# Making w_out's seven operands during attention and the middle experts instead of inside the w_in stage

## The chip, the cores and the metric

The kernel runs on one core of one Trainium2 chip. The metric is the device time of one execution in microseconds (us), as the median of several executions. In the trace of a core PE is the matrix engine (PEld are its weight loads), DVE is VectorE, ACT is ScalarE, POOL is GpSimd, and SP is the queue from which most DMAs are issued.

## What is computed

Three blocks follow each other on 2304 tokens (4 batches of 576). In float32:

```python
def phi(x):                                   # attention, 8 heads of 64, 128 features
    proj = np.einsum('bhsd,md->bhsm', x, omega)
    h = proj - np.sum(x * x, axis=-1, keepdims=True) / 2.0
    return np.exp(h - np.max(h, axis=-1, keepdims=True)) / np.sqrt(m)
kv  = np.einsum('bhsm,bhsd->bhmd', k_p, v);  z = np.sum(k_p, axis=2)
x   = einsum(q_p, kv) / (einsum(q_p, z)[..., None] + 1e-06)
# mixture of experts, top 1 of 8, 512 -> 1024 -> 512
out[mask] = gate_w[mask, None] * (np.maximum(x[mask] @ w1[e], 0.0) @ w2[e])
# dense block, 512 -> 2048 -> 512; w_in and w_out come as 64-bit floats
h = x @ w_in
y = (h * (1.0 / (1.0 + np.exp(-1.702 * h)))) @ w_out
```

## The kernel before

**Attention and experts (to about 405 us).** Attention goes through eight quads (a batch and four heads). Its matrix products hand their results to DVE and ACT and wait for what these return, so PE is kept full with the matmuls of an expert (lines 679 to 764, tiles `m_ps` and `w_ps`) that are laid between them. Each batch goes to one expert, the commonest choice of its tokens. The expert's weights are split into a high and a low part: `wh` by ACT and `wl` by POOL (line 662, `wl<-st,wh`); for the last batch `wl` is made on DVE. DVE makes the low part of the hidden layer (line 697, `h1l`) and scales the result (line 745), and SP stores it to `y_dram`.

**The dense block** uses a seven-product scheme for both matmuls. `first` (line 1068) runs the w_in stage: 24 groups, one for each of eight column pairs j of w_in and each of three sets t of 768 tokens, with seven products of six matmuls each. Its operands are `wi` (two halves of seven combinations of w_in, made by `prep_ins`, line 867) and `y` (the same for a set of tokens, made by `prep_y`, line 929). GELU results go to `g_dram` through three `ob` buffers. `second` (line 1161) runs the w_out stage: nine blocks of 256 tokens, each with seven products of 24 matmuls in the order 1, 7, 5, 6, 2, 4, 3. Its weights `p`, `pw` come from `prep_w` (line 1129), which reads `wo_dram` and splits what it reads. `wo_dram` is filled by `prep_outs` (line 903): for each of eight j it loads two blocks of w_out in 64-bit floats, decodes each with three DVE instructions (line 786), makes four differences (`O_MIX`), and stores seven operands. That is ten DVE instructions for each j. Its results are the tile `pz`, and it begins once set 2 of y exists (line 1260).

**What sets the order.** A `Runner` (line 819) steps the side jobs (`prep_y`, `prep_ins`, `prep_outs`, `prep_w`) once for each step of the main program; the number that a job yields is how many steps it rests. `behind(ins, n)` (line 113) ties an instruction behind the last n ones recorded on its engine, so it stays where it was recorded. All else a scheduler orders by a timeline that it models; after that each engine runs its list in order, and so does the SP queue.

**Room.** `xep` holds the inputs of even batches. `ly` (raw w_in, `yt`, `y0`) is taken when attention has released `att`; `wp` (dec, `wi0`, `wi1`) when batch 2 has passed its first layer. After the last w_in group `wq` takes `wp`'s place and gives two of the five homes `gs` in which `second` keeps its split operands. `marked` (line 1063) records three small matmuls that touch three PSUM banks before the w_in stage.

Of the kernel before, what the change touches and what calls it, by code (L numbers as in the profile page):

```python
# [22 lines left out]
def kernel(  # L23
# [29 lines left out]
    OUT_PACE = 9  # L53
    OUT_GAP = 1
# [152 lines left out]
    xep = tc.alloc_tile_pool(name="xep", bufs=1, side="right")  # L207
    att = tc.alloc_tile_pool(name="att", bufs=1)
# [470 lines left out]
    def moe_gen(b):  # L679
# [3 lines left out]
        for hf in range(2):  # L683
# [46 lines left out]
            for dt in range(KD):  # L730
# [13 lines left out]
                y = yq.tile([P, NH], F32, tag="y", name="y", bufs=3)[:, 0:HS]  # L744
# [122 lines left out]
    def prep_ins():  # L867

        def load(n, j):
            return load_raw(slots["ly"], 0, j + n * NP, 4 if j < 2 else 0)  # L870

        raw = [load(0, 0), load(1, 0)]
        yield IN_PACE
        for j in range(NP):
# [16 lines left out]
            pool, tag = slots["wi"][j % 3]  # L891
            t = pool.tile([P, 14 * HALF], F32R, tag=tag, name="wi", bufs=1)
            w = t.rearrange("p (s o c) -> p s o c", s=2, o=7)
            for o, x in ((slice(0, 2), dec[:, 0:2]), (slice(2, 4), dec[:, 2:4]), (slice(4, 7), mix[:, 0:3])):
                split(w[:, 0, o], w[:, 1, o], x, HOLD)
                yield 1
            wi_t[j] = (w[:, 0], w[:, 1])
# [5 lines left out]
    def prep_outs():  # L903

        raws = slots["raw_o"]

        def load(n, j):
            f = j + n * NP
            nc.sync.dma_start(out=raws[n], in_=w_out[f * P:(f + 1) * P, :])

        load(0, 0)
        load(1, 0)
        yield OUT_PACE
        for j in range(NP):
            z = slots["z"][:, j % 2]
            zi = z.bitcast(I32)
            for n in range(2):
                yield from decoding(zi[:, 2 * n:2 * n + 2].rearrange("p a c -> p (a c)"), raws[n])
                if j + 1 < NP:
                    load(n, j + 1)  # L920
# [3 lines left out]
            nc.sync.dma_start(out=wo_dram[0, :, j], in_=z[:, 0])  # L924
            nc.sync.dma_start(out=wo_dram[1:7, :, j].rearrange("o p d -> p o d"), in_=z[:, 2:8])
            outs[0] += 1
            yield OUT_GAP

# [32 lines left out]
    if True:  # L961
# [11 lines left out]
        done_a = done_m = 0.0  # L973
        a_live = True
# [9 lines left out]
        while a_live:  # L984
# [11 lines left out]
            tick()  # L996
        att_done[0] = True
# [8 lines left out]
        ly = tc.alloc_tile_pool(name="ly", bufs=1)  # L1006
        slots["ly"] = ly
        wp = None
        jobs = Runner(4)
# [8 lines left out]
        y0 = set_tile(ly, 0)  # L1018
        jobs.queue.append(prep_y(0, [y0], 4))
        for n, c in enumerate(Mg):  # L1020
            tick()
            if wp is None and x_done[0] >= B - 1:
                flush()
                xep.release()
                wp = tc.alloc_tile_pool(name="wp", bufs=1)
# [12 lines left out]
        slots["wi"].append((hp, "wi2"))  # L1038
# [24 lines left out]
        def marked(tag):  # L1063

            ps = bank_of(tag, 1, NH)
            nc.tensor.matmul(out=ps, lhsT=y_t[0][0][:, 0, 0, 0:P], rhs=y_t[0][0][:, 0, 0])

        def first(j, t):
# [27 lines left out]
            qs = yq.tile([P, NH], F32, tag="y", name="qs", bufs=3)  # L1096
# [64 lines left out]
        def second(k, gt):  # L1161
            a11, a12, a21, a22 = (gt[:, h, :, i * P:(i + 1) * P] for i in range(2) for h in range(2))

            def made(out, x, y, op):
                behind(nc.vector.tensor_tensor(out=out, in0=x, in1=y, op=op), HOLD if k < 2 else 0)
# [8 lines left out]
            def product(n, ps, start, gs):  # L1174
                gh, gl = gs
                w = wo_t[n]
                for f in range(NP):
                    for m, (x, i) in enumerate(((gh, 0), (gh, 1), (gl, 0))):
# [4 lines left out]
                        if k < 2 and f + m == 0:  # L1183
# [16 lines left out]
            ops = {1: halves_of(a11, HOLD if k < 2 else 0)}  # L1200
# [8 lines left out]
            ops[5] = halves_of(s1)  # L1209
            pa = bank_of("a", 3, HD)  # L1210
# [3 lines left out]
            made(s1, s1, a11, ALU.subtract)  # L1214
            ops[6] = halves_of(s1)
# [43 lines left out]
        def after_group(j, t):  # L1259
            if "z" not in slots and 2 in y_t:  # L1260
                p = ly.tile([P, ZW], F32, tag="yt", name="pz", bufs=1)
                slots["z"] = p[:, 0:16 * HD].rearrange("p (a o d) -> p a o d", a=2, o=8)
                raw = hp.tile([P, DM], I64, tag="raw", name="raw_o", bufs=1)
                slots["raw_o"] = [p[:, 16 * HD:16 * HD + 2 * DM].bitcast(I64), raw]
                jobs.queue.append(prep_outs())
            if (j, t) == (7, 0):
                p = ly.tile([P, SETW], F32R, tag="y0", name="p0", bufs=1)
                jobs.queue += [prep_w(0, p[:, 0:WO], 14), prep_w(1, p[:, WO:2 * WO], 18)]
# [11 lines left out]
            if (j, t) == (5, 2):  # L1280
                jobs.queue.append(prep_w(4, hp.tile([P, WO], F32R, tag="wi2", name="pw", bufs=1), 10))
            if (j, t) in ((7, 1), (5, 2)):
                for _ in range(2):
                    next(blocks[0])
# [25 lines left out]
        jobs.queue += [prep_w(5, p[:, 0:WO], 4, 0), prep_w(6, p[:, WO:2 * WO], 5, 0)]  # L1310
# [20 lines left out]
        ly.release()  # L1331

# [119 lines left out]
```

## Time and profile before

| | |
|---|---|
| median of 3 runs | 788.24 us (787.06 to 791.26) |
| profiled execution, its own time | 792.79 us |
| its span | 790.9 us |
| PE busy | 751.5 us (95%) |
| DVE, ACT, POOL busy | 524.1, 339.6, 131.2 us |

PE is busy nearly throughout, so the time is PE's work plus what PE loses: stretches in which it waits, and stretches in which its clock is granted at half. Where these lie is to be read stage by stage: attention with experts to about 405 us, the w_in stage to 592.8 us, then the w_out stage.

### The profile page before, as it was taken

Reading aid. Unit: us, or ns where it says so; the run is one execution under the profiler, and the core shown is the slowest. Engines: PE = TensorE matmul, PEld = TensorE weight load, DVE = VectorE, ACT = ScalarE, POOL = GpSimd, SP = SyncE. Lnnn points to the kernel's source line nnn. Section 1 sums busy time; section 2 is a strip of 40 time slices with the busy share of each in tenths; the row PEclk is TensorE's granted clock in tenths of the full one; section 3 lists DMA queues with packets and bytes.
Section 4 is the critical chain, followed back from the end, with each engine's and each line's share of the span. In section 5 each row is a group of like instructions: output and inputs, shape, how many; then the busy total and the mean of one; then the engine's idle time right before and its main releaser. Section 6 shows DMA issues by size and latency. Waiting matters only on the chain.

```text
span 790.9 us, 14445 instructions
## 1 busy us (share of the span) xinstructions
PE 751.5 (95%) x5589; PEld 724.4 (92%) x5589; DVE 524.1 (66%) x1178; ACT 339.6 (43%) x643; POOL 131.2 (17%) x78
## 2 busy tenths in 40 slices
PE   7998899999999999799999999998998899999996
PEld 6877799998999999799999999988997899999996
DVE  5877786567764453563679578794267778777761
ACT  5545663345323341541255544443565334444430
POOL 3555386258102240000000000000000000000000
PEclk9999999999999999999999999999999799999998
DMA  6455865267513321644237399896779334444211
GB/s 159 124 142 151 238 185 151 63 177 192 129 32 125 104 65 49 196 125 146 85 109 279 117 314 319 301 316 216 285 259 333 107 128 147 132 135 132 76 27 31
DMA packets 135724, 126.59 MB, mean 160 GB/s; under 512 B 57568, under 2 KB 120288, under 8 KB 134752
## 3 DMA queue, kind: packets, MB, share of 16 engines
q1 hardware_dynamic: 128736, 106.72, 45.0%
q10 hardware_dynamic: 6912, 18.88, 6.3%
q8 instruction: 46, 0.75, 0.4%
q14 instruction: 30, 0.25, 0.1%
HBM read 78.69 MB, written 40.39 MB: 151 GB/s over the span
## 4 chain that ended last, share of the span: by engine, by line
PE 68%; DMA 11%; DVE 11%; ACT 4%; issue 3%; SPq 1%; POOL 1%; ACTq 0%; DVEq 0%; POOLq 0%
PE m_ps L126 17%; PE qa L1179 12%; PE qa L1078 9%; PE qm L1179 6%; PE w_ps L126 4%; DMA g_dram<-g 3%; PE pb L1179 3%; PE num L431 3%; DMA m<-in_k_dram 2%; PE qm L1078 2%; PE qu L1078 2%; PE kv_ps L389 2%; DMA st<-in_moe_w_dram 2%; DMA m<-in_q_dram 1%; PE pr L331 1%
## 5 line engine op out<-in xcount | busy, mean ns | idle before, releaser
L1078 PE MATMUL qa<-y,wi 128*128 128x384 f32 x576 | 110.6, 339 | 3.7 <-DVE g L863 2.3
L1078 PEld LDWEIGHTS qa<-y,wi 128*128 128x128 f32 x576 | 100.8, 188 | 6.9 <-DVE g L863 4.0
L126 PE MATMUL m_ps<-xh,wh 128*128 128x288 f32 x256 | 79.5, 311 | 4.3 <-DVE h1l L697 4.3
L126 PE MATMUL m_ps<-xh,wl 128*128 128x288 f32 x256 | 77.2, 302 | 0.0
L126 PE MATMUL m_ps<-xl,wh 128*128 128x288 f32 x256 | 77.1, 301 | 0.0
L662 POOL TENSOR_TENSOR wl<-st,wh 128x1024 fp32r<-128x1024 f32 x23 | 54.5, 2377 | 90.8 <-ACT wh L660 90.7
L697 DVE SCALAR_TENSOR_TENSOR h1l<-m_ps,h1h 128x288 fp32r<-128x288 f32 x64 | 29.0, 455 | 61.2 <-ACT h1h L694 60.9
L346 DVE TENSOR_REDUCE small<-pr 128x4 f32<-128x512 f32 (+1 forms) x80 | 51.1, 639 | 13.9 <-PE pr L338 6.7
L660 ACT ACTIVATE wh<-st 128x1024 fp32r<-128x1024 f32 (+1 forms) x33 | 33.9, 1033 | 47.8 <-DMA st<-in_moe_w_dram 23.4
L126 PEld LDWEIGHTS m_ps<-xh,wh 128*128 128x128 f32 x256 | 49.2, 192 | 5.2 <-DVE h1l L697 4.7
L694 ACT ACTIVATE h1h<-m_ps 128x288 fp32r<-128x288 f32 x64 | 25.8, 405 | 59.9 <-PE m_ps L126 59.8
L126 PEld LDWEIGHTS m_ps<-xl,wh 128*128 128x128 f32 x256 | 49.3, 193 | 0.1
L126 PEld LDWEIGHTS m_ps<-xh,wl 128*128 128x128 f32 x256 | 49.2, 192 | 0.0
L126 PE MATMUL m_ps<-h1h,wh 128*128 128x288 f32 x160 | 48.5, 304 | 0.0
L126 PE MATMUL m_ps<-h1l,wh 128*128 128x288 f32 x160 | 47.8, 299 | 0.0
L126 PE MATMUL m_ps<-h1h,wl 128*128 128x288 f32 x160 | 47.5, 298 | 0.0
L1179 PE MATMUL qa<-p,p 128*128 128x256 f32 x360 | 46.8, 288 | 0.0
L1179 PE MATMUL qa<-p,gs 128*128 128x256 f32 x360 | 45.6, 282 | 1.1 <-DVE gs L817 0.8
L1179 PEld LDWEIGHTS qa<-p,p 128*128 128x128 f32 x360 | 45.5, 196 | 0.0
L1179 PEld LDWEIGHTS qa<-p,gs 128*128 128x128 f32 x360 | 43.9, 189 | 1.5 <-DVE gs L817 1.0
L431 PE MATMUL num<-kv,qpT 128*128 128x65 f32 (+1 forms) x320 | 39.0, 265 | 2.2 <-ACT qpT L419 1.4
L431 PEld LDWEIGHTS num<-kv,qpT 128*128 128x128 f32 (+1 forms) x320 | 36.2, 183 | 5.4 <-ACT qpT L419 2.7
(211 smaller groups left out, 1823.8 us busy)
## 6 DMA issues: line engine op xcount, KB each, us to landing
g_dram<-g ACTq DMA_DIRECT2D x48, 384.0 KB, 4.2
st<-in_moe_w_dram SPq DMA_DIRECT2D x31, 512.0 KB, 3.9
pg<-g_dram SPq DMA_DIRECT2D x10, 1024.0 KB, 5.7
raw<-in_moe_w_in_dram SPq DMA_DIRECT2D x16, 512.0 KB, 4.9
gt<-g_dram SPq DMA_DIRECT2D x8, 1024.0 KB, 6.1
wo_dram<-pz SPq DMA_DIRECT2D x8, 768.0 KB, 4.9
p<-wo_dram SPq DMA_DIRECT2D x6, 1024.0 KB, 7.2
yt<-y_dram SPq DMA_DIRECT2D x12, 384.0 KB, 5.7
```

The source lines that it names most:

```text
L126: ins = nc.tensor.matmul(out=ps, lhsT=a, rhs=b, start=start and n == 0, stop=stop and n == 2)
L331: nc.tensor.matmul(out=ps[:, :, h2], lhsT=xT[:, (2 * pr + h2) * 2 + t0 // 2], rhs=wbd)
L346: nc.vector.tensor_reduce(out=pm, in_=ps[:, :w], axis=AX.X, op=ALU.max, negate=on_act)
L389: nc.tensor.matmul(out=kv_ps[:, h, :], lhsT=kp[j // 2][:, j % 2, h2, :], rhs=vm[:, h, t, :], start=(t == 0), stop=False,)
L431: nc.tensor.matmul(out=ps[:n, c, h2, :], lhsT=lhsT, rhs=kv[:, h, :])
L660: nc.scalar.activation(out=hi[:, :, s], in_=st[:, :, s], func=ACTF.Copy)
L662: eng.tensor_tensor(out=lo[:, :, s], in0=st[:, :, s], in1=f32(hi)[:, :, s], op=ALU.subtract)
L694: nc.scalar.activation(out=hh[:, f], in_=ps, func=ACTF.Relu)
L697: nc.vector.scalar_tensor_tensor(out=hl[:, f], in0=ps, scalar=0.0, in1=f32(hh[:, f]), op0=ALU.max, op1=ALU.subtract)
L1078: ins = nc.tensor.matmul(out=ps, lhsT=w[:, a, ks], rhs=y[:, b, kk], start=start and kk + m == 0, stop=kk == 1 and m == 2, skip_group_check ...
L1179: ins = nc.tensor.matmul(out=ps, lhsT=x[:, f], rhs=w[i][:, f], start=start and f + m == 0, stop=f == NP - 1 and m == 2, skip_group_check=True,
```

## The change

`prep_outs` now runs during attention and the experts of batches 0 to 2, from the moment batch 0 has passed its first layer. It has a pool `wz` of its own (tags a and b, 16 KB of each partition), one operand tile instead of two, loads tied to places in SP's list, and a rest of 5 steps after each j. Since `wz` takes room, `ly` is allocated only when `xep` is released; `prep_y` of set 0 therefore starts when batch 2 has passed its first layer and all expert weights are staged, and `prep_ins` waits for `prep_outs`. `wz` later holds `wi` of j = 0, 3, 6, and then two of the homes `gs`, which are so free one group before the w_in stage ends. In the first w_out block the sixth operand is made before product 1 is issued (`sixth`), and two more steps of the block are taken after group (6, 2). `prep_w` rests shorter (14, 18, 10, 4, 5 become 10, 14, 7, 3, 4). The third w_out block is tied in order as the first two are. `marked` is tied behind the matmul before it; `y` becomes a tile of 288 columns, and `qs` moves to a pair of buffers in `hp`.

```diff
-    OUT_PACE = 9
-    OUT_GAP = 1
+    OUT_PACE = 5
+    IN_FIRST = 5
...
+    wz = tc.alloc_tile_pool(name="wz", bufs=1)
     att = tc.alloc_tile_pool(name="att", bufs=1)
...
     def prep_ins():
...
+        while outs[0] < NP:
+            yield 1
         raw = [load(0, 0), load(1, 0)]
-        yield IN_PACE
+        yield IN_FIRST
...
     def prep_outs():
-        raws = slots["raw_o"]
+        z = wz.tile([P, 8 * HD], F32, tag="a", name="z", bufs=1).rearrange("p (o d) -> p o d", o=8)
+        zi = z.bitcast(I32)
+        raws = wz.tile([P, 2, DM], I64, tag="b", name="raw_o", bufs=1)
         def load(n, j):
             f = j + n * NP
-            nc.sync.dma_start(out=raws[n], in_=w_out[f * P:(f + 1) * P, :])
+            behind(nc.sync.dma_start(out=raws[:, n], in_=w_out[f * P:(f + 1) * P, :]), 2)
...
-        yield OUT_PACE
+        yield 8
         for j in range(NP):
-            z = slots["z"][:, j % 2]
-            zi = z.bitcast(I32)
             for n in range(2):
...
-            for o, a, b, op in O_MIX:
+            for i, (o, a, b, op) in enumerate(O_MIX):
+                if j + 1 < NP and not i % 2:
+                    load(i // 2, j + 1)
                 behind(tt(nc.vector, z[:, o], z[:, a], z[:, b], op), HOLD)
                 yield 1
...
-            yield OUT_GAP
+            yield OUT_PACE
...
+        jobs = Runner(4)
+        jobs.queue.append(prep_outs())
...
             tick()
+            if x_done[0]:
+                jobs()
...
-                slots["wi"] = [(wp, "wi0"), (wp, "wi1")]
+                slots["wi"] = [wi_pair, wi_home(wp, "wi1")]
...
-                slots["go"] = jobs.queue.extend([prep_ins(), prep_y(1, home1, 4)])
+                slots["go"] = jobs.queue.extend([prep_y(0, [set_tile(ly, 0)], 4), prep_ins(), prep_y(1, home1, 4)])
...
+            def sixth():
+                made(s1, s1, a11, ALU.subtract)
+                ops[6] = halves_of(s1)
+            if not k:
+                yield
+                sixth()
+                yield
             pa = bank_of("a", 3, HD)
             product(1, pa, True, ops[1])
             c1 = kept(pa, "c1")
             yield
-            made(s1, s1, a11, ALU.subtract)
-            ops[6] = halves_of(s1)
+            if k:
+                sixth()
...
+            if (j, t) == (6, 2):
+                gs_homes.extend(wz.tile([P, GSW], F32R, tag=tag, name="gs", bufs=1) for tag in ("a", "b"))
...
-        gs_homes += [wq.tile([P, GSW], F32R, name=f"gs{i}") for i in range(2)]
```

Three places show how the lists of the engines moved.

DVE, the first decoding of w_out in the changed kernel (`z` and `raw_o` are its tiles; `small`, `mx`, `qp`, `kp` belong to attention). The kernel before has at this place:

```order
L367 TENSOR_TENSOR kp<-pr,mx 128x512
L346 TENSOR_REDUCE small<-pr 128x4
L355 TENSOR_TENSOR small<-small,sq 128x4
L355 TENSOR_TENSOR mx<-small,sq 128x4
L367 TENSOR_TENSOR qp<-pr,mx 128x512
```

and the changed kernel:

```order
L368 TENSOR_TENSOR kp<-pr,mx 128x512
L347 TENSOR_REDUCE small<-pr 128x4
L789 TENSOR_SCALAR z<-raw_o 128x512
L356 TENSOR_TENSOR small<-small,sq 128x4
L794 SCALAR_TENSOR_TENSOR z<-raw_o,z 128x512
L356 TENSOR_TENSOR mx<-small,sq 128x4
L798 SCALAR_TENSOR_TENSOR z<-raw_o,z 128x512
L368 TENSOR_TENSOR qp<-pr,mx 128x512
```

One instruction on `z` now stands between nearly every two of attention's. PE's list answers to this: the same transposes of attention stand behind more expert matmuls than before, 24 more at the 44th transpose `tx<-ident,xn` (456 where there were 432), 46 more at the 48th (514 where there were 468), and 3 fewer at the last. POOL's list is the same in both kernels.

PE, the three marker matmuls into `qn`, `qu` and `qt`. Before, they stand among the matmuls of the expert of batch 2:

```order
L126 MATMUL w_ps<-h1h,wl_4079 128x288
L1066 MATMUL qn<-y_3932 128x384
L1066 MATMUL qu<-y_3932 128x384
L1066 MATMUL qt<-y_3932 128x384
L126 MATMUL w_ps<-h1h,wh_4078 128x288 x3
```

Now they stand behind the last matmul of batch 3:

```order
L126 MATMUL w_ps<-h1h,wl_4708 128x288
L1085 MATMUL qn<-y_4656 128x384
L1085 MATMUL qu<-y_4656 128x384
L1085 MATMUL qt<-y_4656 128x384
L1097 MATMUL qa<-y_4656,wi 128x384 x6
```

On ACT and DVE the splits of `y0` moved with them, from beside batch 2 to beside batch 3.

DVE at the border between the w_in and w_out stages, from the last sum of the w_in stage (`g<-qa,qs`) on; `gs` and `p` are operands and weights of the first w_out block, and `s` minus `pg` is the sixth operand's sum. Before:

```order
L863 TENSOR_TENSOR g<-qa,qs 128x384
L817 TENSOR_TENSOR p_6708<-p_6708 128x1024 x3
L817 TENSOR_TENSOR gs_6875<-s_6711,gs_6875 128x1024
L817 TENSOR_TENSOR p_6878<-pg,p_6878 128x1024
L817 TENSOR_TENSOR pw<-pw 128x1024 x2
L1165 TENSOR_TENSOR s_6711<-s_6711,pg 128x1024
L817 TENSOR_TENSOR p_6517<-pg,p_6517 128x1024
L817 TENSOR_TENSOR gs_6876<-s_6711,gs_6876 128x1024
```

Now:

```order
L818 TENSOR_TENSOR gs<-s_6717,gs 128x1024
L864 TENSOR_TENSOR g<-qa,qs 128x384
L818 TENSOR_TENSOR p_6714<-p_6714 128x1024
L1184 TENSOR_TENSOR s_6717<-s_6717,pg 128x1024
L818 TENSOR_TENSOR p_6714<-p_6714 128x1024
L818 TENSOR_TENSOR pw<-pw 128x1024
L818 TENSOR_TENSOR gs<-s_6717,gs 128x1024
```

The fifth operand's split moved ahead of the last sum of the stage, and the sixth's from the tenth place behind that sum to the fifth.

## Rows read from the trace of the kernel before

**Rows 1.** The page, its first part: busy us, share of the span, instructions.
```profile
PE 751.5 (95%) x5589; PEld 724.4 (92%) x5589; DVE 524.1 (66%) x1178; ACT 339.6 (43%) x643; POOL 131.2 (17%) x78
```
**Rows 2.** PE in order of time, batch 2's expert: start, us, instruction [idle before].
```profile
329.86 0.45 PE L1066 MATMUL qn<-y 128*128 128x384 f32 x1 [0.98 <-ACT y L816]
...
331.10 0.66 PE L126 MATMUL w_ps<-h1h,wh 128*128 128x288 f32 x3 [0.45 <-ACT h1h L694]
334.96 0.61 PE L126 MATMUL m_ps<-xh,wh 128*128 128x288 f32 x1 [3.20 <-DVE h1l L697]
```
**Rows 3.** ACT in order of time, the same stretch.
```profile
328.96 0.84 ACT L816 ACTIVATE y<-yt 128x768 fp32r<-128x768 f32 x1 [6.20 <-DMA yt<-y_dram]
```
**Rows 4.** Stretches: length, busy PE, PEld, DVE, ACT, POOL (instructions), granted clock, DMA share, GB/s.
```profile
335.00:339.20 4.20, 4.20 (x17) 4.20 (x18) 4.20 (x6) 1.56 (x3) 0.00 (x0) 0.50 0.19 63
537.70:540.60 2.90, 2.90 (x9) 2.90 (x10) 2.87 (x6) 1.34 (x2) 0.00 (x0) 0.50 0.14 47
613.40:619.10 5.70, 5.70 (x27) 5.70 (x28) 5.70 (x6) 2.32 (x3) 0.00 (x0) 0.50 0.19 64
626.00:629.30 3.30, 3.30 (x18) 3.30 (x17) 2.76 (x3) 1.06 (x1) 0.00 (x0) 0.50 0.50 131
```
**Rows 5.** PE in order of time, the w_in stage.
```profile
496.77 2.37 PE L1078 MATMUL qa<-y,wi 128*128 128x384 f32 x12 [0.91 <-DVE g L863]
...
531.66 2.79 PE L1078 MATMUL qa<-y,wi 128*128 128x384 f32 x12 [1.10 <-ACT wi L816]
536.30 0.62 PE L1078 MATMUL qm<-y,wi 128*128 128x384 f32 x2 [1.85 <-ACT wi L816]
537.71 1.65 PE L1078 MATMUL qm<-y,wi 128*128 128x384 f32 x4 [0.78 <-DVE wi L817]
```
**Rows 6.** PE in order of time, the first two w_out blocks.
```profile
601.87 0.51 PE L1179 MATMUL qa<-p,gs 128*128 128x256 f32 x2 [0.36 <-ACT gs L816]
603.13 2.88 PE L1179 MATMUL qa<-p,gs 128*128 128x256 f32 x22 [0.76 <-DVE gs L817]
...
611.87 0.39 PE L1179 MATMUL qm<-p,p 128*128 128x256 f32 x1 [1.56 <-ACT p L816]
613.32 2.72 PE L1179 MATMUL qm<-p,p 128*128 128x256 f32 x11 [1.06 <-DVE p L817]
...
625.33 4.39 PE L1179 MATMUL qm<-p,gs 128*128 128x256 f32 x22 [1.90 <-DVE gs L817]
```
**Rows 7.** Stretches, tile pz alone: length, busy DVE (instructions), clock, DMA share, GB/s.
```profile
441.00:543.00 102.00, 41.29 (x80) 0.98 0.80 275
```
**Rows 8.** Stretches of attention with experts, columns as in rows 4.
```profile
182.00:200.00 18.00, 16.35 (x162) 15.38 (x161) 16.90 (x49) 9.54 (x17) 15.80 (x8) 1.00 0.80 175
200.00:241.00 41.00, 41.00 (x357) 38.92 (x355) 27.82 (x106) 13.52 (x33) 2.38 (x1) 1.00 0.26 68
242.00:300.00 58.00, 58.00 (x472) 56.71 (x472) 25.30 (x75) 20.50 (x38) 18.99 (x8) 1.00 0.32 98
```
**Rows 9.** POOL in order of time, attention with experts.
```profile
165.71 2.11 POOL L254 TENSOR_TENSOR m<-m 128x1152 f32<-128x1152 f32 x1
...
184.95 2.38 POOL L662 TENSOR_TENSOR wl<-st,wh 128x1024 fp32r<-128x1024 f32 x1
...
196.35 2.39 POOL L662 TENSOR_TENSOR wl<-st,wh 128x1024 fp32r<-128x1024 f32 x1 [0.94 <-ACT wh L660]
```
**Rows 10.** DVE in order of time, attention with experts.
```profile
166.43 1.41 DVE L582 SCALAR_TENSOR_TENSOR rr<-eq,ixf 128x5 f32<-128x5 f32 x1
...
185.91 0.69 DVE L346 TENSOR_REDUCE small<-pr 128x4 f32<-128x512 f32 x1
```
**Rows 11.** Line 582 alone: duration in ns, shortest, median, longest; first and last start.
```profile
L582 DVE SCALAR_TENSOR_TENSOR rr<-eq,ixf x4: 149/161/1410, 86.5 to 317.5; 128x5 f32<-128x5 f32 x4
```
**Rows 12.** The chain that ended last, one piece of an expert: start, us, what.
```profile
253.53 1.65 PE m_ps L126 x12
```
**Rows 13.** DVE groups: busy us, mean ns of one, idle before.
```profile
L817 DVE TENSOR_TENSOR p<-p 128x1024 fp32r<-128x1024 f32 x12 | 14.1, 1218 | 0.3 <-DMA g_dram<-g 0.3
```

More of the change, by code (lines that the diff above doesn't have):

```diff
@@ L1005 @@
             nc.scalar.activation(out=wg[:, 0, 0:1], in_=total, func=ACTF.Gelu_apprx_sigmoid)
[L1006 to L1009, printed above, removed]
+        ly = wp = None
         SETW = 14 * 2 * NH
@@ L1017, with wi_home, taken, wi_pair @@
         home1 = []
-        y0 = set_tile(ly, 0)
-        jobs.queue.append(prep_y(0, [y0], 4))
-        for n, c in enumerate(Mg):
+        def wi_home(pool, tag):
+            def taken():
+                w = pool.tile([P, 14 * HALF], F32R, tag=tag, name="wi", bufs=1).rearrange(
+                    "p (s o c) -> p s o c", s=2, o=7
+                )
+                return w[:, 0], w[:, 1]
+            return taken
+        def wi_pair():
+            return tuple(
+                wz.tile([P, 8 * HALF], F32R, tag=tag, name="wi", bufs=1).rearrange("p (o c) -> p o c", c=HALF)[:, 0:7]
+                for tag in ("a", "b")
+            )
+        for c in Mg:
             tick()
@@ L1065, in marked @@
             ps = bank_of(tag, 1, NH)
-            nc.tensor.matmul(out=ps, lhsT=y_t[0][0][:, 0, 0, 0:P], rhs=y_t[0][0][:, 0, 0])
+            behind(nc.tensor.matmul(out=ps, lhsT=y_t[0][0][:, 0, 0, 0:P], rhs=y_t[0][0][:, 0, 0]), 1)
         def first(j, t):
@@ L1095, in first @@
             product(7, pq, True)
[L1096 removed]
+            qs = hp.tile([P, NH], F32, tag="qs", name="qs", bufs=2)
             nc.scalar.activation(out=qs, in_=pq, func=ACTF.Copy)
@@ L1164, in made @@
             def made(out, x, y, op):
-                behind(nc.vector.tensor_tensor(out=out, in0=x, in1=y, op=op), HOLD if k < 2 else 0)
+                behind(nc.vector.tensor_tensor(out=out, in0=x, in1=y, op=op), HOLD if k < 3 else 0)
                 return out
@@ L1182, in product @@
                         )
-                        if k < 2 and f + m == 0:
+                        if k < 3 and f + m == 0:
                             tc.keep_in_program_order(ins)
@@ L1199, in second @@
             last = k == NT // (2 * P) - 1
-            ops = {1: halves_of(a11, HOLD if k < 2 else 0)}
+            ops = {1: halves_of(a11, HOLD if k < 3 else 0)}
             yield
@@ L1259, in after_group @@
         def after_group(j, t):
[L1260 to L1265, printed above, removed]
             if (j, t) == (7, 0):
                 p = ly.tile([P, SETW], F32R, tag="y0", name="p0", bufs=1)
-                jobs.queue += [prep_w(0, p[:, 0:WO], 14), prep_w(1, p[:, WO:2 * WO], 18)]
+                jobs.queue += [prep_w(0, p[:, 0:WO], 10), prep_w(1, p[:, WO:2 * WO], 14)]
                 gs_homes.append(p[:, 2 * WO:2 * WO + GSW])
@@ L1280, in after_group @@
             if (j, t) == (5, 2):
[L1281 to L1284, printed above, removed]
+                jobs.queue.append(prep_w(4, hp.tile([P, WO], F32R, tag="wi2", name="pw", bufs=1), 7))
+            if (j, t) == (6, 2):
+                gs_homes.extend(wz.tile([P, GSW], F32R, tag=tag, name="gs", bufs=1) for tag in ("a", "b"))
+            for _ in range({(7, 1): 2, (5, 2): 2, (6, 2): 2}.get((j, t), 0)):
+                next(blocks[0])
         live = None
```

28 lines of the change are left out of this document (14 added, 14 removed).

## The prediction

> **What bounds the kernel now.** The page's first part comes first: PE is busy 95% of the span [rows 1], so nothing that only moves work on another engine pays by itself. What can be won is what PE loses, so the views after it are PE in order of time, for the gaps with what ended each, and tables by stretch, for the granted clock. They show three places. In the expert of batch 2 PE waits three times within 6 us: first for the markers, whose operand `y` ACT had not split, then for `h1h` and `h1l`, which stood behind the splits of `y` [rows 2]; ACT itself had idled 6.20 us there for the load of `yt` [rows 3]. In the w_in stage PE waits late for `wi` and for sums on DVE [rows 5], in the stretch where DVE also makes the w_out operands, 41.29 us of DVE time [rows 7]. In the first two w_out blocks it waits for operands and weights that DVE and ACT split too late [rows 6]. Three of the gaps are followed by stretches with the clock granted at 0.50, that is at 1.2 instead of 2.4 GHz, in which PE works all the time and so loses half [rows 4].
>
> **The batch 2 stall.** The markers and the splits of `y0` leave this place. The gaps are 0.98 + 0.45 + 3.20 = 4.6 us, and the stretch after them at half clock is 4.20 us long, so it costs 2.1. Gain 6.7. Nothing is late there next: what stands between is one expert's own matmuls, splits and `wl`, in the order that ran without a gap before. Bounds: 4.6 (another gap keeps the clock low) to 6.7.
>
> **The w_in stage.** All 80 instructions on `pz` go, 41.29 us of DVE in 102 us, and with them 16 loads and 16 stores in a stretch where the DMA engines are busy 0.80 of the time [rows 7]. The gaps for `wi` and for sums, 0.91 + 1.10 + 1.85 + 0.78 = 4.6 us [rows 5], had nothing else in front of them on DVE, and the half-clock stretch at 537.7 costs 2.90 / 2 = 1.45. Gain 6.1. What holds it at zero instead would be `g` buffers that wait for their stores (the DMA share says this gets easier too). Bounds 3 to 7.
>
> **The border.** The sixth operand's split, for which PE waited at 603.13, moves from the tenth place behind the last w_in sum to the fifth; at 1.22 us for a split [rows 13] that is some 6 us earlier, and its home is free a group earlier. So 0.36 + 0.76 go. The weights that PE waited for at 611.87 and 613.32 (1.56 + 1.06) now stand behind less, and the second block's operand at 625.33 (1.90) had DVE's whole backlog in front of it. With the two half-clock stretches, 5.70 / 2 + 3.30 / 2 = 4.5, all of it is 10.1 us [rows 4, 6]. Not all goes: the last weight load still can start only when the last w_in group has let go of set 2, and product 3's operand now stands on DVE behind a sum that needs product 4. I leave one split on PE's path, 1.2, and one half-clock stretch, 1.65, and take 7.3. Bounds 3.5 to 10.1. The shorter rests of `prep_w`, the tied third block, the new homes of `qs` and `y` and the extra steps go together at nothing beyond this: they move splits by a step or two where PE works on products made already, and if that cover is gone their price is in the bounds.
>
> **The batch 3 expert.** `y0` now costs DVE 11 instructions of at most 1.22 us each [rows 13] beside batch 3, where before it was set 1's four sums. They are placed between evictions of PSUM; I take 0.5 us, bounds 0 to 3.
>
> **Attention with experts, the price.** The same 80 instructions, 5.16 us for each j, now stand one by one between attention's, from the second half of attention on. DVE has no work to spare at first: from 182 to 200 us it is busy 16.90 of 18 us, and PE already loses 1.65 [rows 8]. The place of the first ten is after the reduction at 185.91 [rows 10]. There PE's list has 24 more expert matmuls ahead of the same transposes; twelve take 1.65 us [rows 12], so they fill 3.3 us, and DVE's idle 1.1 us more. Of the 5.16 us 0.8 is left for PE to wait. The next three j cost 15.5 us, against an idle 13.2 us of DVE from 200 to 241 and 22 more matmuls (3.0 us): nothing left. The last four cost 20.6 against 32.7 idle from 242 to 300: nothing left. SP's queue carries the loads and stores of `z` ahead of expert weights, transposes and y stores; a store waits for ten DVE instructions, and what is behind it was ordered a step or more early, so I price that at nothing up to 2 us.
>
> But DVE does not only lose its own time there. The instruction `rr` takes 161 ns at the median; once it took 1410 [rows 11], and that one began at 166.43 while POOL worked on a product from 165.71, and ended at 167.84, as POOL's ended at 167.82 [rows 9, 10]. `rr` reads two operands from SBUF, as eight of the ten instructions of a j do; attention's own, which read PSUM, stand in this stretch at their usual durations. Before the change the 80 instructions ran where POOL was idle. Now the first ten meet six POOL instructions, from 184.95 to the one at 196.35 [rows 9], on average 1.98 us each [rows 8]. Each can hold one instruction on `z`, and all of attention queues behind that. The first is met with 0.7 us to go; for the other five I take off 0.25 us for the short instruction in between: 0.7 + 5 x 1.73 = 9.3 us, on PE's path, since the matmuls drawn forward are used up. One more POOL instruction lies in the stretch to 241 (1.2, half of it) and eight in that to 300, where the idle DVE and expert matmuls cover the wait but for some 0.6. Bounds 0 to 33 (all of 6 x 1.98 + 2.38 + 18.99).
>
> The Trainium skill, page "SBUF — State Buffer", section "Who interferes with whom", says that VectorE and GpSimd share one port pair as an exclusive lock, taken by a VectorE instruction with two SBUF inputs, so that the later one blocks until the first has finished. The `rr` row agrees with it, 1410 against 149 ns. By an ordinary sum of DVE's time without such a lock the whole change would come out at the first rival's time.
>
> **The sum.** Gains 6.7 + 6.1 + 7.3 = 20.1; costs 0.5 + 0.8 + 9.3 + 1.2 + 0.6 = 12.4; net 7.7 us. The profiled execution took 792.79 us, so 785.1; it stands 0.58% above the median of the runs, so on the median's scale 785.1 x 788.24 / 792.79 = **780.6 us**. About 0.5% is what a measurement of this kernel can tell from no change: below 784.3 is faster, above 792.2 slower.
>
> **Rivals.**
> 1. *POOL holds nothing that matters.* The scheduler's places for `z` fall into POOL's gaps, or POOL's splits slip instead. For it: POOL's work is only 2.38 us from 200 to 241 [rows 8]. Against it: it is busy 15.80 of 18 us where the first ten stand. Then costs are 1.3, net 18.8: 774.0, or 769.6 on the median's scale.
> 2. *The borders keep half of their waits.* `wi` and the first w_out weights are late for their loads rather than for DVE, and the gaps re-form. For it: four of these nine gaps name ACT, which waits on its inputs. Against it: DVE is busy throughout the stretches named. Gains fall by (6.1 + 7.3) / 2 = 6.7, net 1.0: 791.8, or 787.2.
> 3. *Slower: DVE held at every meeting.* One mechanism, from 185.91 us on: each of the 15 POOL instructions holds one of `z`, its whole length is PE's, because the expert matmuls next in PE's list need `h1l`, which queues behind `z` on DVE. It decides once the wait, 2.4 us, is longer than the matmuls in hand, 1.65 us for one group of twelve [rows 12]. Costs 0.5 + 0.8 + 33.3 = 34.6, net a loss of 14.5: 807.3, or 802.7. Against it: two PSUM banks and attention's own matmuls give more in hand than one group.
>
> That the change fails to do what it says is excluded by the order of the lists; only its times are open.
>
> **How the numbers follow.** Forecast 0.50, rival 1 0.24, rival 2 0.16, rival 3 0.10. The range 768 to 790 takes in rivals 1 and 2 with about 2 to 3 us beyond each and leaves out rival 3 and the far ends of the bounds. Faster: most of the forecast (0.40), rival 1 (0.24), a little of rival 2 (0.02), 0.66. Same: 0.09 + 0.13 = 0.22. Slower: 0.10 + 0.02 = 0.12.
>
> **What would show it.** In the profile after: no `y<-yt` wait on ACT and no gap at the markers in the expert of batch 2; `z` instructions near 186 us that last 1 to 2.4 us instead of 0.4 to 0.7, and new PE gaps of some 10 us in all between 185 and 205 us; `wi` never the releaser of PE; at most one gap of over 1 us at the w_out border. The prediction is wrong in its price if `z` keeps its durations beside a busy POOL, and in its gains if the half-clock stretches of [rows 4] come back at the w_in stage's end.

## The result, and the profile after

The change makes the kernel slower: median 799.88 us (798.06 to 802.50, four runs) against 789.05 us (787.06 to 791.26), a ratio of 1.0139 (95% interval 1.0097 to 1.0181). Forecast were 780.6 us and a range of 768 to 790. The profiled execution took 802.50 us; its span is 800.7 us, 9.8 more than the 790.9 of before. The two spans divide at the first product of the w_in stage and at the first of the w_out stage. The boundaries of the changed kernel, PE in order of time (start, us, instruction):

```profile
420.77 0.51 PE L1097 MATMUL qa<-y,wi 128*128 128x384 f32 x2
...
601.09 0.28 PE L1198 MATMUL qa<-p 128*128 128x256 f32 x1
```

| stage | before, us | after, us | difference | forecast |
|---|---|---|---|---|
| attention and experts | 405.39 | 420.77 | +15.4 | +5.7 |
| w_in stage | 187.4 | 180.3 | -7.1 | -6.1 |
| w_out stage | 198.1 | 199.6 | +1.5 | -7.3 |

The forecast of a stage is the sum of the prediction's terms for it (-6.7 + 0.5 + 0.8 + 9.3 + 1.2 + 0.6 for the first). The w_in stage came as forecast, as far as the sum goes. The two others carry the error: 9.7 us in attention and 8.8 us in the w_out stage.

**Attention.** Part of the 15.4 us has nothing to do with the change. POOL's product on `m`, which both kernels reach before anything differs, starts at 165.71 before [rows 9] and 4.0 us later now:

```profile
169.67 2.11 POOL L255 TENSOR_TENSOR m<-m 128x1152 f32<-128x1152 f32 x1
```

The cause is the clock: this execution has half clock for 6.8 us at 48.1 and again at 85.6 us (the table by stretch below), the kernel before only for 3.4 us at 83.2. It is a matter of chance, as the last section shows. The other 11.4 us lie behind it. Chance has a part in these too: six of the experiments below change only what comes later and run attention and the experts in the same order, and from this product on `m` to the w_in stage they take 7.7 to 10.3 us longer than the kernel before, whose single profile is of an execution 3.7 us above its median. PE's waits there, PE in order of time with the idle time before each:

```profile
189.78 0.66 PE L418 MATMUL tq<-ident,qp 128*128 128x128 f32 x4 [1.55 <-DVE xl L461]
199.13 1.09 PE L418 MATMUL tq<-ident,qp 128*128 128x128 f32 x4 [4.62 <-DVE qp L368]
...
267.17 0.27 PE L454 MATMUL small<-ident,xn 64*128 64x64 f32 x1 [1.08 <-DVE mx L356]
...
275.80 1.08 PE L390 MATMUL kv_ps<-vm,kp 128*128 128x65 f32 x8 [1.22 <-issue]
301.79 0.63 PE L418 MATMUL tq<-ident,qp 128*128 128x128 f32 x4 [2.80 <-DVE qp L368]
```

Three groups of waits, at 188 to 199, 266 to 276 and 299 to 303 us. DVE in order of time shows what the first one is made of:

```profile
191.72 2.12 DVE L789 TENSOR_SCALAR z<-raw_o 128x512 int32<-128x512 int32 x1 [0.31 <-DMA raw_o<-in_moe_w_out_dram]
193.76 0.15 DVE L356 TENSOR_TENSOR small<-small,sq 128x4 f32<-128x4 f32 x1
193.87 2.72 DVE L794 SCALAR_TENSOR_TENSOR z<-raw_o,z 128x512 int32<-128x512 int32 x1
196.51 0.15 DVE L356 TENSOR_TENSOR mx<-small,sq 128x4 f32<-128x4 f32 x1
196.62 1.76 DVE L798 SCALAR_TENSOR_TENSOR z<-raw_o,z 128x512 int32<-128x512 int32 x1
198.30 0.68 DVE L368 TENSOR_TENSOR qp<-pr,mx 128x512 f32<-128x512 f32 x1
```

POOL in order of time, the same stretch:

```profile
191.44 2.12 POOL L255 TENSOR_TENSOR m<-m 128x1152 f32<-128x1152 f32 x1
193.50 2.54 POOL L663 TENSOR_TENSOR wl<-st,wh 128x1024 fp32r<-128x1024 f32 x1
196.00 1.83 POOL L260 TENSOR_TENSOR m<-m 128x576 f32<-128x576 f32 x1
```

Each of the three decodes begins while POOL works and ends 0.3 to 0.6 us after POOL's instruction (193.84 behind 193.56, 196.59 behind 196.04, 198.38 behind 197.83). Attention's own small instructions keep their 0.15 us, and `qp`, for which PE waits, stands behind all three. The groups of `z` by form show the usual duration, the median of the three numbers, beside the held one:

```profile
L789 DVE TENSOR_SCALAR z<-raw_o x16: 406/422/2119, 191.7 to 321.8; 128x512 int32<-128x512 int32 x16
...
L798 DVE SCALAR_TENSOR_TENSOR z<-raw_o,z x16: 671/682/2753, 196.6 to 323.6; 128x512 int32<-128x512 int32 x16
```

Nine of the 80 instructions are held, by 12.7 us in all (duration less the median of its group, summed); all nine meet an instruction of POOL and end 0.3 to 0.6 us after it. In the later groups of waits it is again `z`, held or waiting, on DVE in order of time:

```profile
266.62 0.43 DVE L789 TENSOR_SCALAR z<-raw_o 128x512 int32<-128x512 int32 x1 [3.78 <-DMA wo_dram<-z]
...
271.82 2.75 DVE L798 SCALAR_TENSOR_TENSOR z<-raw_o,z 128x512 int32<-128x512 int32 x1
...
293.98 2.67 DVE L798 SCALAR_TENSOR_TENSOR z<-raw_o,z 128x512 int32<-128x512 int32 x1
...
297.51 1.67 DVE L789 TENSOR_SCALAR z<-raw_o 128x512 int32<-128x512 int32 x1
```

The first row is something else: the tile `z` could not be written again before its store had landed, and DVE stood for 3.78 us. On SP the two stores stand behind two loads of expert weights. Before these SP had stood 2.6 us until DVE had chosen the expert (line 591), and the stores then took 6.9 and 7.6 us to land:

```profile
257.12 1.09 SPq L639 DMA_DIRECT2D st<-in_moe_w_dram  x2
...
259.67 0.58 SPq L926 DMA_DIRECT2D wo_dram<-z  x1
260.29 0.43 SPq L927 DMA_DIRECT2D wo_dram<-z  x1
```

The table by stretch (length, busy PE, PEld, DVE, ACT, POOL with instructions, granted clock, DMA share, GB/s) has the half-clock stretches of the changed kernel, each a little inside its ends (a last one, at the kernel's end, stands there before too and is left out):

```profile
48.20:54.80 6.60, 6.60 (x24) 5.43 (x25) 4.96 (x17) 2.81 (x7) 5.11 (x4) 0.50 0.11 25
85.70:92.40 6.70, 6.70 (x40) 6.04 (x41) 4.85 (x25) 2.86 (x9) 0.00 (x0) 0.50 0.50 121
198.40:205.00 6.60, 5.87 (x32) 5.74 (x33) 6.53 (x18) 2.20 (x4) 2.38 (x1) 0.50 0.63 183
270.10:273.30 3.20, 3.20 (x15) 3.20 (x14) 3.20 (x7) 1.37 (x2) 2.16 (x1) 0.50 0.56 142
304.20:307.40 3.20, 3.20 (x15) 3.20 (x14) 1.48 (x6) 1.60 (x2) 0.00 (x0) 0.50 0.99 359
628.50:631.70 3.20, 3.20 (x15) 3.20 (x16) 2.16 (x2) 1.01 (x1) 0.00 (x0) 0.50 0.00 0
652.30:659.00 6.70, 5.14 (x24) 5.14 (x25) 4.99 (x5) 1.06 (x1) 0.00 (x0) 0.50 0.39 126
```

Those of [rows 4] are gone at 335 and 537 us; three new ones stand behind the waits in attention, and the two of the w_out stage are there again, later. In the experts of batches 2 and 3 PE's gaps fell from 6.1 to 2.3 us (gaps over 0.3 us, summed), and no half clock is left between 310 and 628 us.

**w_in.** The gaps over 0.3 us that [rows 5] show for `wi` fell to these two, and the half clock went:

```profile
544.07 0.61 PE L1097 MATMUL qa<-y,wi 128*128 128x384 f32 x2 [1.10 <-ACT wi L817]
545.03 2.00 PE L1097 MATMUL qa<-y,wi 128*128 128x384 f32 x10 [0.36 <-DVE wi L818]
```

The whole stage, before and now, in the columns of the table by stretch, shows that PE is also busy for 4.3 us less, of which half clock explains 1.5:

```profile
405.39:592.76 187.37, 181.07 (x1010) 177.24 (x1009) 132.68 (x241) 97.69 (x186) 0.00 (x0) 0.99 0.76 262
420.77:601.09 180.32, 176.77 (x1010) 174.44 (x1009) 98.40 (x161) 99.00 (x187) 0.00 (x0) 1.00 0.52 184
```

**w_out.** The five waits of [rows 6], 5.6 us, are gone. In their place stand three, 5.9 us, later in the first three blocks:

```profile
620.16 2.90 PE L1198 MATMUL qa<-p,p 128*128 128x256 f32 x22 [0.86 <-DVE p L818]
628.44 4.36 PE L1198 MATMUL qm<-p,gs 128*128 128x256 f32 x22 [1.81 <-DVE gs L818]
653.86 5.06 PE L1198 MATMUL qm<-p 128*128 128x256 f32 x22 [3.27 <-DVE p L818]
```

### The profile page after: what moved, and what is told of

Read it like the earlier page. It is cut to its first block, busy times and chain, and to the rows that moved or that the text cites. A ratio compares the mean times of both kernels' runs of the same rounds, so it can differ in the third digit from the quotient of the medians.

```text
span 800.7 us, 14405 instructions
## 1 busy us (share of the span) xinstructions
PE 755.4 (94%) x5589; PEld 728.7 (91%) x5589; DVE 530.4 (66%) x1178; ACT 340.4 (43%) x643; POOL 132.5 (17%) x78
## 4 chain that ended last, share of the span: by engine, by line
PE 45%; DVE 5%; DMA 3%; issue 1%; ACT 1%; DVEq 0%; ACTq 0%; SPq 0%
PE qa L1198 12%; PE qa L1097 11%; PE qm L1198 7%; PE m_ps L126 3%; PE pb L1198 3%; PE qm L1097 3%; PE qu L1097 2%; PE w_ps L126 2%; DMA g_dram<-g 2%; PE qn L1097 1%; PE qt L1097 1%; DVE y L818 1%; DVE p L818 1%; DMA gt<-g_dram 1%; DVE gs L818 1%
## 5 line engine op out<-in xcount | busy, mean ns | idle before, releaser
L347 DVE TENSOR_REDUCE small<-pr 128x4 f32<-128x512 f32 (+1 forms) x80 | 51.1, 639 | 10.3 <-PE pr L339 3.9
```

Source lines behind the costliest of these rows:

```text
L347: nc.vector.tensor_reduce(out=pm, in_=ps[:, :w], axis=AX.X, op=ALU.max, negate=on_act)
```

## The experiments

A ratio is always to the kernel before, run beside the kernel in the same job. The changed kernel's own is 1.0139.

### Does POOL hold DVE, or is it DVE's time?

Two runs move the price in two ways. The first begins the job 12 steps later, behind most of POOL's run of instructions:

```diff
-        yield 8
+        yield 20
         for j in range(NP):
```

> The changed kernel with prep_outs resting 20 steps instead of 8 before its first j, so that the first j stands behind POOL's six instructions in a row. Theory A, POOL holds DVE: the three long instructions on z of j = 0 (excess 4.8 us) are short, the gaps of 1.55 and 4.62 us at 188 to 199 us and the half clock behind them (3.4) shrink to what the kernel before has there (1.4): about 8 us less, 791 to 793; the instructions on z that meet wl from 262 us on stay long. Theory B, plain DVE time: the same 5.16 us a j are missing wherever they stand, and with the end of the job later the time stays at 798 or more.

The second takes POOL's eight `wl` of batch 1 and eight of batch 2 away from it; ACT makes a copy in their place, without the subtraction:

```diff
-                eng.tensor_tensor(out=lo[:, :, s], in0=st[:, :, s], in1=f32(hi)[:, :, s], op=ALU.subtract)
+                if b in (1, 2) and eng is nc.gpsimd:
+                    nc.scalar.activation(out=lo[:, :, s], in_=st[:, :, s], func=ACTF.Copy)
+                else:
+                    eng.tensor_tensor(out=lo[:, :, s], in0=st[:, :, s], in1=f32(hi)[:, :, s], op=ALU.subtract)
```

> The changed kernel in which the low part of the expert weights of batches 1 and 2 is not made by POOL but is a plain copy on ACT (this leaves out the subtraction), so that POOL's long instructions are gone from 174 us on but for those on m and hl. Theory A, POOL holds DVE: no instruction on z is long from 205 us on and the gaps of 1.22 us at 274 and 2.80 us at 299 go with their half clock (3.4): 6 to 10 us less, 790 to 794, if ACT's extra 15 us (1.04 each) find room. Theory B, plain DVE time or late stores of z: the gaps stay, 798 or more.

Measured: 12 steps later 793.34 us, ratio 1.0040 (1.0009 to 1.0070); without POOL's `wl` 786.14 us, ratio 0.9944 (0.9909 to 0.9979). Plain DVE time is out: the second run has every instruction of the job on DVE, and 16 copies of 1.04 us more on ACT, and is 2% faster than the changed kernel, more than was expected of it. Its held time is 1.9 us, in three instructions that meet `m` and `hl`. The first run missed its number in part: three of the first ten instructions still met a `wl` and a gap of 3.43 us stayed. And its held time was larger than the changed kernel's, 16.0 us against 12.7, while its first w_in product came at 409.63 us against 420.77; 4.6 us of that are the clock before the product on `m`, which here starts at 165.07, and 6.5 are not. So the held time itself is not the price. It costs what PE has not in hand at the place where it falls.

Three more runs separate the two places. One makes batch 2's `wl` on DVE (1.23 us each) instead of POOL:

```diff
-                eng = nc.vector if (b * 2 * NW + c) in SPLIT_D or b == B - 1 else nc.gpsimd
+                eng = nc.vector if (b * 2 * NW + c) in SPLIT_D or b >= B - 2 else nc.gpsimd
```

> The changed kernel with the low part of batch 2's expert weights made by DVE (1.23 us each, eight of them, 9.8 us) instead of POOL, as batch 3's already is. Theory A, POOL holds DVE: the held instructions on z of j = 4 to 6 (excess 6.8 us at 272 to 298 us) return to 0.42 and 0.68 us, the gaps at 274 and 299 us go (1.2, 2.8, 0.5, and the half clock behind them, 3.4): 4 to 7 us less than the changed kernel although DVE has 9.8 us more to do; the gaps at 188 to 199 us stay. Theory B, plain DVE time: 9.8 us more on DVE makes it slower, at or over the changed kernel. Theory C, the wait of z for its own stores: the gaps at 266 to 269 us stay (2.0 us) and only they matter there: within 2 us of the changed kernel.

One begins the job with a rest of 32 steps (`yield 8` becomes `yield 32`):

> The changed kernel with a rest of 32 steps before the first j, so that the job begins when POOL's run of instructions up to 206 us is over. Theory A, POOL holds DVE: no instruction of j = 0 to 2 is long, the gap of 3.4 us that was left at 198 us with 20 steps goes too, so 2 to 5 us less than with 20 steps; j = 3 to 6 still meet POOL's eight wl. Theory B, plain DVE time: the same as with 20 steps within 1.5 us, or more, since all of the job is later.

One does both:

> Both of the others: a rest of 32 steps before the first j, and batch 2's wl on DVE. Theory A: no instruction on z is held anywhere, so the time is that of the run in which ACT took POOL's part, or a little more for DVE's 9.8 us: a ratio of 0.993 to 1.000 to the kernel before. Theory B, plain DVE time: 1.004 or more.

Measured: 794.33 us, ratio 1.0036 (1.0001 to 1.0071) with batch 2's `wl` on DVE; 788.41 us, 0.9965 (0.9930 to 0.9999) with 32 steps; 791.90 us, 1.0015 (0.9978 to 1.0052) with both. In the first, DVE has 9.8 us more to do and the kernel is 1% faster: no instruction of j = 2 to 7 is held any more, and the wait of 2.80 us before 301.79 shrank to 1.14. The second is the shortest edit of the three, with the largest effect: one number, 24 steps later, takes 1.7% off and ends level with the kernel before or just under it. Its groups of `z`, to be read against those above:

```profile
L789 DVE TENSOR_SCALAR z<-raw_o x16: 417/427/1644, 198.5 to 335.2; 128x512 int32<-128x512 int32 x16
...
L798 DVE SCALAR_TENSOR_TENSOR z<-raw_o,z x16: 669/682/693, 210.2 to 336.6; 128x512 int32<-128x512 int32 x16
```

Three instructions are held there, by 2.4 us in all, and from 180 to 300 us no wait of PE is over 0.7 us; the w_in stage begins at 405.54 us. That is as before the change and not earlier: the job now ends in batch 2's expert, and PE has new waits for `h1h` and `h1l` there, 5.2 us from 339 to 354. That the eight `wl` of batch 2 are hardly met either is luck of the phase, not design: they still run on POOL from 247 to 292 us. With both edits there was nothing more to free, and DVE's 9.8 us are only a cost; the interval overlaps the other's.

`z` waits for its stores in these runs too (6.5 us in five waits with 32 steps), and PE loses little by it there. In the run with `wl` on ACT it does cost: POOL has no instruction near, DVE stands for the stores with `h1l` behind, and PE waits for that, with 3.4 us of half clock after it. The two rows, DVE and PE in order of time:

```profile
262.26 0.43 DVE L792 TENSOR_SCALAR z<-raw_o 128x512 int32<-128x512 int32 x1 [4.59 <-DMA wo_dram<-z]
...
263.84 0.61 PE L126 MATMUL m_ps<-xh,wh 128*128 128x288 f32 x1 [3.08 <-DVE h1l L701]
```

So the wait for the stores is a second cause beside POOL. A second tile for `z` would take it alone away; that was not tried, and what it would gain stays open.

### Why did the border gain nothing?

The first suspects were the third block's tie and the rests. One run unties the third block alone, one ties the fourth as well (`k < 3` becomes `k < 2`, or `k < 4`, in its three places), one takes the old rests of `prep_w`:

> The changed kernel with only the third w_out block untied again (made, the first operand and the pinned matmuls for k below 2, as before). Theory A, the tie: the wait of 3.27 us for a split of the third block's first operand at 650.59 us and most of the half clock behind it (6.8 us, worth 3.4) come from the tied order, so both go: 5 to 6.7 us less than the changed kernel, 793 to 795. Theory B, DVE's backlog: the wait only takes another place within two blocks, 798 or more.

> The changed kernel with the fourth w_out block tied as well (k below 4). Theory A: the wait of 3.27 us at 650 us is made of the fourth block's two sums (1.22 us each, and 0.48 of waiting for its load) that the scheduler put between the tied sums of the third block; tied too, they stand behind, and the wait falls to 0.5 us or less, with its half clock: 4 to 6 us less than the changed kernel, unless a like wait opens at the next border between tied and untied blocks. Theory B, the splits come too slowly whatever their order: the wait stays over 2 us, within 1.5 us of the changed kernel.

```diff
-                jobs.queue += [prep_w(0, p[:, 0:WO], 10), prep_w(1, p[:, WO:2 * WO], 14)]
+                jobs.queue += [prep_w(0, p[:, 0:WO], 14), prep_w(1, p[:, WO:2 * WO], 18)]
...
-        jobs.queue += [prep_w(5, p[:, 0:WO], 3, 0), prep_w(6, p[:, WO:2 * WO], 4, 0)]
+        jobs.queue += [prep_w(5, p[:, 0:WO], 4, 0), prep_w(6, p[:, WO:2 * WO], 5, 0)]
```

> The changed kernel with the rests of prep_w as before (14, 18, 10, 13, 10, 4, 5). Theory A, DVE's total work between 597 and 631 us sets the waits of the first two w_out blocks: the three waits change place, the sum of the w_out gaps stays within 2 us, 798 to 802. Theory B, the shorter rests bring the weights' splits ahead of operands that PE needs sooner: the wait of 1.81 us at 626 goes, 795 to 797.

Measured: untied 795.57 us, ratio 1.0055 (1.0025 to 1.0084); the fourth tied 800.72 us, 1.0149 (1.0097 to 1.0202); old rests 798.41 us, 1.0110 (1.0047 to 1.0173). Where the third block is untied, its wait is gone, and the w_out stage takes 197.3 us against 199.6. But the wait has only moved into the second block, whose 1.81 us grow to 5.72, so the stage waits 0.6 us longer in all; what it gains lies in the half clock, at which PE works 4.1 us instead of 8.6. Theory B had the wait right, theory A nearly the time. PE in order of time:

```profile
619.09 2.90 PE L1198 MATMUL qa<-p,p 128*128 128x256 f32 x22 [0.86 <-DVE p L818]
627.18 0.50 PE L1198 MATMUL qm<-p,gs 128*128 128x256 f32 x2 [2.31 <-ACT gs L817]
631.09 4.73 PE L1198 MATMUL qm<-p,gs 128*128 128x256 f32 x22 [3.41 <-DVE gs L818]
```

The old rests bring two waits of [rows 6] back (1.54 and 1.06 us) in place of the 0.86, and keep the two others. Tying the fourth block did what its last half-sentence feared: the wait of the third fell to 1.94 us, and 3.27 us opened in the fourth. The run with every block tied, together with the rest of 32 steps, shows the rule:

> A rest of 32 steps before the first j and all nine w_out blocks tied. If a wait opens only where tied and untied blocks meet, this has none behind the second block: 0.987 to 0.993. If the scheduler's order is better than the written one in the later blocks, it is over the run with four blocks tied, 0.995 or more.

The first three of its waits from the third block on, PE in order of time:

```profile
636.15 2.90 PE L1198 MATMUL qm<-p 128*128 128x256 f32 x22 [1.94 <-DVE p L818]
658.51 3.92 PE L1198 MATMUL qm<-p,gs 128*128 128x256 f32 x22 [1.94 <-DVE gs L818]
682.34 3.87 PE L1198 MATMUL qm<-p,p 128*128 128x256 f32 x22 [1.94 <-DVE p L818]
```

It took 805.94 us, ratio 1.0213 (1.0169 to 1.0257); the same 1.94 us stand in all seven blocks from the third on. The written order costs 1.94 us in each block that it binds from the third on. In the last bound block 1.3 us come on top, since the scheduler lays sums of the next, free block between. In the changed kernel these are the first and third row here, on DVE in order of time; PE waits for the last row:

```profile
646.57 1.22 DVE L1184 TENSOR_TENSOR s<-gt 128x1024 f32<-128x1024 f32 x1 [0.48 <-DMA gt<-g_dram]
...
649.18 1.22 DVE L818 TENSOR_TENSOR p<-s,p 128x1024 fp32r<-128x1024 f32 x1
650.32 1.22 DVE L1184 TENSOR_TENSOR gt<-gt 128x1024 f32<-128x1024 f32 x1
...
652.59 1.22 DVE L818 TENSOR_TENSOR p<-pg,p 128x1024 fp32r<-128x1024 f32 x1
```

With the fourth block tied and 32 steps the ratio is 1.0003 (0.9976 to 1.0030), over that of 32 steps alone: the tie gives back what the later start wins.

> A rest of 32 steps before the first j and the fourth w_out block tied. Theory A for both: the two gains add up, a ratio of 0.988 to 0.994 to the kernel before. If only the later start counts: 0.9965.

Three runs asked after the two waits that the tie does not explain, 0.86 and 1.81 us. In two the last two weights lose their subtraction on DVE: once their low part is a copy on ACT, once they get none.

> The changed kernel in which the low parts of the last two w_out weights (those of products 4 and 3) are a plain copy on ACT instead of a subtraction on DVE (this leaves out the subtraction): four instructions of 1.22 us, 4.9 us, leave DVE at the border of the w_out stage. Theory A, DVE's backlog up to 631 us sets the waits of the first three blocks: the sum of the gaps from 601 to 655 us falls from 5.9 us to 3 or less and the half clock behind them with it, 3 to 6 us less than the changed kernel. Theory B, the tied order of PE and DVE sets them: the waits of 1.81 and 3.27 us stay, within 1.5 us of the changed kernel.

> The changed kernel in which the last two w_out weights (products 4 and 3) get no low part at all (this leaves out four subtractions of 1.22 us; the matmuls read the unsplit weight in its place): 4.9 us less for DVE at the border, nothing more for ACT, and the order of everything else kept. Theory A, DVE's backlog sets the waits of 0.86 and 1.81 us in the first two blocks: both go, the one at 650 us stays; 3 to 5 us less than the changed kernel with the half clock. Theory B, PE gives a home or a sum back too late and the chain of splits behind it sets the wait: the 1.81 stays or grows, within 1.5 us of the changed kernel.

The third takes one home of five away (`% 5` becomes `% 4`):

> The changed kernel with four homes for split operands in a ring instead of five. Theory A, the wait of 1.81 us at 626 us comes from a home that PE gives back late: with one home less each such operand starts a product (2.9 us) later, so the waits of the first three blocks, 5.9 us in sum, grow to 9 or more. Theory B, the chain of splits on ACT and DVE sets it, not the homes: within 1.5 us of 5.9.

The copy on ACT told nothing: 799.00 us, ratio 1.0104 (1.0033 to 1.0174), but `gs` then stood behind the copies on ACT, so the load had only changed engine. Without the four low parts it is 793.97 us, 1.0058 (1.0029 to 1.0087), and the w_out stage takes 195.0 us. Two waits stay, PE in order of time:

```profile
619.51 2.89 PE L1201 MATMUL qm<-p,gs 128*128 128x256 f32 x22 [1.63 <-DVE gs L818]
643.39 4.30 PE L1201 MATMUL qm<-p 128*128 128x256 f32 x22 [3.27 <-DVE p L818]
```

So DVE's backlog made the 0.86, and 0.2 of the 1.81; most of the rest of the 4.6 us is half clock, 6 us less of it here, which also changes by chance (last section). With four homes (a single run, 800.34 us) the first three blocks wait less, 3.8 us, and later ones more; neither theory gave that, as the scheduler had put the list in another order. Which step of the chain makes the 1.6 us in the second block stays open.

### Do the border edits gain anything, and is there a better kernel?

Both runs have the rest of 32 steps. One has the border as before the change (by the edit below, with two blocks tied and the old rests), the other all its edits but the third tie.

```diff
-            if not k:
-                yield
-                sixth()
-                yield
             pa = bank_of("a", 3, HD)
...
-            if k:
-                sixth()
+            sixth()
...
-            for _ in range({(7, 1): 2, (5, 2): 2, (6, 2): 2}.get((j, t), 0)):
+            for _ in range({(7, 1): 2, (5, 2): 2}.get((j, t), 0)):
```

> A rest of 32 steps before the first j, and the w_out border as it was before: the sixth operand in its old place, no steps after group (6, 2), the old rests, two blocks tied. Theory A, the border edits only moved the waits and the third tied block added one: the w_out stage is 1 to 3 us shorter than in the run with the rest of 32 steps alone, a ratio of 0.992 to 0.996. Theory B, the border edits gained what the forecast gave them: it is 5 us or more longer, 1.002 or more.

> A rest of 32 steps before the first j, and the third w_out block untied. If the gains of the two single runs add up: 2 us less than with the rest alone, 0.992 to 0.996.

Old border: 784.52 us, ratio 0.9941 (0.9917 to 0.9964). Edits without the tie: 786.16 us, 0.9944 (0.9917 to 0.9971). They are equal within the noise, and so are their w_out stages, 197.4 and 197.1 us. The old border has three of its five old waits; the two for the sixth operand, 0.36 and 0.76 us, are gone without the edit that was to remove them:

```profile
607.18 0.39 PE L1198 MATMUL qm<-p,p 128*128 128x256 f32 x1 [1.53 <-ACT p L817]
608.63 2.72 PE L1198 MATMUL qm<-p,p 128*128 128x256 f32 x11 [1.06 <-DVE p L818]
620.65 4.39 PE L1198 MATMUL qm<-p,gs 128*128 128x256 f32 x22 [1.86 <-DVE gs L818]
```

The edits gain nothing, the tie loses some 2 us (788.41 with it, 786.16 without), by half clock and not by longer waits, and both kernels beat the one before by 0.6% and the changed one by 2%.

## Why the prediction was wrong

- **The w_in stage, right in sign, and in size partly by luck.** Forecast 6.1 us, measured 7.1, and 6.8 to 8.0 in all fifteen experiments. But PE's waits fell by 2.7 us where 4.6 were counted ("`wi` never the releaser of PE" failed: 1.10 and 0.36 us remain). The half clock gave the 1.5 that was counted. The other 2.8 us are PE's busy time at full clock, a term that the prediction does not have and that no run explains.
- **The batch 2 stall, right.** Forecast 6.7 less 0.5. In the experts of batches 2 and 3 gaps fell by 3.8 us, and 10.2 us of half clock went. PE had worked in 7.6 us of these and stood in the others, so they were worth 3.8: 7.6 in all.
- **The first ten instructions on `z`, right in mechanism, near in size by luck.** Forecast 0.8 + 9.3 us. Measured were 1.55 + 4.62 less 1.38 that was there before, and half clock in which PE worked 6.0 us, worth 3.0: 7.8. The mechanism is that of the forecast: decodes of 1.76 to 2.72 us beside POOL, behind them attention. But four of the ten were held, by 5.2 us in all, where six were counted; of the 24 expert matmuls set against them only 8 stand ahead of the transposes that waited at 199.13; and the half clock was not in the sum. The Trainium skill, page "SBUF — State Buffer", section "Who interferes with whom", names `tensor_scalar` too among the instructions that can take the port pair shared with GpSimd, although it reads one operand; the trace agrees, 2119 ns against 422, where I had counted only the eight with two.
- **The failing step in attention** is the term for the other seven j: "eight in that to 300, where the idle DVE and expert matmuls cover the wait but for some 0.6", with 1.2 for the stretch before. Measured are 6.5 us of gaps over 0.3 us from 266 to 303 us and 6.8 us of half clock, worth 3.4, 9.9 in all against 1.8. DVE's idle time is an average over 58 us. A held instruction puts 2 us in one piece in front of `mx`, `qp` or `h1l`, and PE's list waits for just these. The wait for `z`'s own stores, priced at nothing up to 2 us, was part of it: DVE stood 7.0 us in four such waits, and 2.0 of PE's 6.5 us, at 266 to 269, stand behind the longest. The half clock was counted where waits went and forgotten where new ones came. With 4.0 by chance, 7.8, 9.9 and the 7.6 gained, 1.3 of the 15.4 us are in none of these.
- **The failing step at the border** is "I leave one split on PE's path, 1.2, and one half-clock stretch, 1.65, and take 7.3", with "the tied third block" at nothing. The waits named did go, but what came behind them was not looked at: PE met the next late operands, 0.86 and 1.81 us, and 3.27 us in the tied block, which without the tie stood in the second. That is 5.9 us of waits and 4.3 of half clock, 10.2 in all, against the 2.9 that the prediction left and the 10.1 that it counted before. The runs put the edits at zero and the tie at a loss of some 2 us.
- **The rivals.** The slower one had the right sign and, at 802.7 us, nearly the time, but not for its reason alone: nine of the 15 meetings were held, not all, and half of the error lies at the border. The second had the border re-form its gaps, as it did, but for late loads, where the runs show the order of the splits.
- Two readings of the prediction are off with little effect: it says that three gaps are followed by half clock, while [rows 4] and its own sum have four, and its 1.98 us a POOL instruction is the mean of the eight in that stretch, while the six that it counts take 2.17.
- Of the profile's +9.8 us, 4.0 are chance on the side of the changed kernel; what chance did in the profile of the kernel before is not known. The medians, 10.8 us apart, do not rest on these two executions.

## What to carry to other kernels

Before moving vector work into another stage, lay its instructions beside GpSimd's in time, not beside the mean idle time of its own engine: the same 80 instructions made this kernel 1.7% faster when they were moved, by a start 24 steps later, to where GpSimd mostly rests or happens not to be met. When a wait on the path is taken away, look up the next operand that the engine needs and when it is ready, for a gain ends there. Price half clock for the new gaps as well as for the old ones, and test each part of a bundle of edits alone, since here one number, the start of the job, made nearly all of the loss.

## What the runs showed of the hardware that was not expected

- **The same gap is followed by half clock in some executions only.** All profiles have a wait of 1.1 to 1.4 us near 46.5 us, where the kernels do not differ. Behind it 4 of 17 show 3.4 or 6.8 us at 0.50, this changed kernel among them, the kernel before not. In the run with `wl` on ACT the three waits of the w_out stage (0.86, 1.81, 3.28 us) have no half clock behind them, and the stage takes 195.7 us against the changed kernel's 199.6 with the same waits.
- **POOL is held too.** Three `wl` that began while DVE was in an instruction on `z` took 2.54, 2.59 and 2.88 us instead of 2.4, and an `m` 1.83 instead of 1.42.
- **DVE gets in between two POOL instructions that follow at once.** The decode at 193.87 waited for one of them, not for both.
